# Scores in causal blocks and states in channel blocks on the column groups of the matmul array

## The chip, the cores and the metric

The kernel runs on one core of a Trainium2 chip. The core has a matrix engine (PE in the profile; its weight loads are shown as PEld), a vector engine (DVE), a scalar engine (ACT), GpSimd (POOL) and SP, which here issues all the kernel's DMAs. The metric is the device time of one execution in microseconds; lower is better.

## The reference, cut to what matters

The program is a gated linear recurrence (4 batches, 8 heads, 768 steps, 48 channels per head), followed by a feed-forward network with a product of two branches. In the recurrence, a state of 48 x 48 per head is turned and shrunk by a complex gate at each step, receives the outer product of k and v, and is read by q.

```python
mag = np.sqrt(a_re * a_re + a_im * a_im)
scale = np.minimum(mag, 0.999) / (mag + 1e-06)
a_re_n, a_im_n = (a_re * scale, a_im * scale)
for t in range(S):
    ar, ai = (a_re_n[:, :, t, :, None], a_im_n[:, :, t, :, None])
    new_re = ar * S_re - ai * S_im
    new_im = ar * S_im + ai * S_re
    kv = np.einsum('bhd,bhe->bhde', k[:, :, t], v[:, :, t])
    S_re, S_im = (new_re + kv, new_im)
    y[:, :, t] = np.einsum('bhd,bhde->bhe', q[:, :, t], S_re)
# then, with x = y as (3072, 384):
h = (x @ w1) * (x @ w2) @ w3
return (h @ w_out).astype(np.float32)
```

## The kernel before

The kernel computes the recurrence in closed form. The running product of the gates is taken out of the sum: q is multiplied by it, k is divided by it, and both become vectors of 96 numbers per step and head (real and imaginary parts of 48 channels). Then y is the causal part of a score matrix (k against q) times v, plus q times a state that is carried from chunk to chunk. A chunk is C = 128 steps. A unit u is half a batch: all 8 heads (H) over TT = 384 steps, so UC = 3 chunks; there are NU = 8 units.

For each unit, `gates` (from line 541) computes the gates' products with a long chain of operations that alternates between ACT and DVE. Its last product for k is gR, line 634. `move` (line 648) then copies the results from a layout of 3 tiles of 128 partitions into QL and KL, where the 96 channels of one head lie on 96 partitions. The recurrence's work on PE comes in pieces, listed by `pieces` (line 1005):

- `turn` transposes k's two parts (line 671); ACT copies the result to KT (line 673).
- `state` (line 714) multiplies, for each head, KT (128 steps x 96 channels as weights) with v, whose head is padded to 64 columns (line 721), and adds the result to the carried state T (line 728); after the last chunk of a unit T is scaled (line 734). In the second unit of a batch the last chunk needs no state, so a batch has 5 state chunks.
- `scores` (line 676) is called twice for a chunk, with x = 0 and 1, for 4 heads each: one product per head of 128 keys (weights) with 128 queries (line 683). DVE copies the part that the mask `causal` allows into A (line 685); A was cleared once, so what is not allowed stays zero.
- `outputs` (line 691) multiplies A with v and T with q, in pieces of 32 output channels that go to four different ranges of 32 output partitions (line 710). The head's 48 channels and 16 zeros make two such pieces; QUADS says which pieces of two neighbouring heads are summed in one place. An even head has its 48 channels first, an odd head has them last. ACT copies the sum to xT (line 712).

The v of a unit is loaded with one DMA into vr (line 517, `load_v`, called in `load_qkv`); ACT spreads it into the padded V with two copies (line 524, `spread_v`, called in `gates`). vr has one buffer, V has two.

The feed-forward network of a unit (lines 744 to 750, and 795 or 831 for its output) follows one unit behind. `unit` (line 1026) interleaves on PE its pieces with the recurrence's pieces, and issues a step of the next unit's `gates` after each. PE's order is thus written out by hand (`manual_schedule`, line 1042). On the other engines and on SP the framework's planner orders the instructions, by its own estimates of cost and by priority; the copies out of PE's results are marked as of high priority. At the start, the weights of the network are converted from double precision, and w3 and w_out are multiplied together (`fuse`, line 968, into eight accumulators in PSUM, two of them from the pool of the scores). In later units `check_weights` (line 899) loads weights once more ("look") and checks ranges on ACT (lines 918 to 921).

Of the kernel before, what the change touches and what calls it, by code (L numbers as in the profile page):

```python
# [13 lines left out]
U16 = mybir.dt.uint16  # L14
BF = mybir.dt.bfloat16
# [359 lines left out]
def kernel(  # L375
# [55 lines left out]
    LO, HI = 32, D - 32  # L431
    LN_EPS = math.log(1e-6)
# [16 lines left out]
    three = fast.enter_context(tc.tile_pool(name="three", bufs=3))  # L449
    ps_s = fast.enter_context(tc.tile_pool(name="ps_s", bufs=2, space=PSUM))  # L450
# [6 lines left out]

    Ab = [singles.tile([P, H, C], FP, name=f"A{i}") for i in range(2)]
# [3 lines left out]
    causal = singles.tile([P, C], I32, name="causal")  # L462
    nc.gpsimd.iota(causal, pattern=[[1, C]], base=0, channel_multiplier=-1)
    nc.vector.tensor_scalar(out=causal, in0=causal, scalar1=0, scalar2=None, op0=OP.is_ge)
# [37 lines left out]
    def load_qkv(u):  # L502
        b, h = divmod(u, 2)
        if "q" not in g_t.get(u, {}):
            take_qk(u)
        g = g_t[u]
        load_rows(g["k"], kt, u)
        load_rows(g["q"], qt, u)
        if u:
            load_v(u)  # L510
# [9 lines left out]
    def spread_v(u):  # L520
        vr = g_t[u]["vr"].rearrange("p c (h two d) -> p c h two d", two=2, d=D)
        V = Vb[u % 2].rearrange("p c (h two) e -> p c h two e", two=2)
        for i, e0 in enumerate((0, 64 - D)):
            nc.scalar.copy(out=V[:, :, :, i, e0:e0 + D], in_=vr[:, :, :, i])
# [16 lines left out]
    def gates(u, split):  # L541
# [64 lines left out]
        if u:  # L606
            spread_v(u)
# [68 lines left out]
    def scores(u, c, x):  # L676
# [4 lines left out]
        sc = ps_s.tile([P, n, C], FP, tag="sc", name="sc")  # L681
        for j in range(n):
            nc.tensor.matmul(out=sc[:, j], lhsT=KL[:, x * n + j, w], rhs=QL[:, x * n + j, w], start=True, stop=True)  # L683
        with tc.high_priority():
            masked[:] = [nc.vector.copy_predicated(out=A[:, x * n:(x + 1) * n], data=sc,  # L685
                                      mask=causal.rearrange("p (h t) -> p h t", h=1).to_broadcast([P, n, C]))]


    QUADS = [q for h in range(0, H, 2) for q in ([(h, 0)], [(h, 1), (h + 1, 0)], [(h + 1, 1)])]

    def outputs(u, c):
# [9 lines left out]
        for i, q in enumerate(QUADS):  # L701
            f, j = divmod(i, 4)
            o = y[32 * j:32 * j + 32, f]
            got = [(V[:, hd, 32 * e:32 * e + 32], A[:, hd]) for hd, e in q]
            if not first:
                got += [(T[:, hd, 32 * e:32 * e + 32], QL[:, hd, w]) for hd, e in q]
# [6 lines left out]

    def state(u, c):

        KT, V = KT_t.pop((u, c)), Vb[u % 2][:, c]
        n = u % 2 * UC + c
        T = T_t.get((u // 2, n))
        kv = ps_v.tile([2 * D, H, 64], FP, tag="v", name="kv")
        for hd in range(H):  # L720
            nc.tensor.matmul(out=kv[:, hd], lhsT=KT[:, hd].rearrange("p d x f -> p (d x f)"), rhs=V[:, hd],  # L721
                             start=True, stop=True)
        Tn = three.tile([2 * D, H, 64], FP, tag="T", name="T")
        with tc.high_priority():
            if T is None:
                nc.scalar.copy(out=Tn, in_=kv)
            else:
                add = nc.vector.tensor_tensor(out=Tn, in0=kv, in1=T, op=OP.add)  # L728
# [3 lines left out]
        if c == UC - 1:  # L732
            rho = L_t[u][1][:, :, TT:TT + 1].to_broadcast([2 * D, H, 64])
            nc.vector.tensor_tensor(out=Tn, in0=Tn, in1=rho, op=OP.mult)
        T_t[u // 2, n + 1] = Tn

# [231 lines left out]
    def fuse(f, j):  # L968
        if not sums:
            sums.extend([ps_s.tile([P, DM], FP, tag="sc", name="f") for _ in range(2)] +  # L970
# [71 lines left out]
    with tc.manual_schedule(engines={mybir.EngineType.PE}):  # L1042
# [9 lines left out]
        for f in range(KF):  # L1052
# [5 lines left out]
            if f == VLOAD:  # L1058
                load_v(0)
            if f >= KF - 2:  # L1060
# [8 lines left out]
        spread_v(0)  # L1069
# [10 lines left out]
        for i, p in enumerate(pieces(0)):  # L1080
# [4 lines left out]
            if i == 0:  # L1085
                for f in work[:2]:
                    f()
                load_qkv(1)
            for _ in range(5 if i == 0 else i >= 6):
# [17 lines left out]
        for u in range(1, NU):  # L1107
            steps = gates(u + 1, False) if u + 1 < NU else iter(())
# [49 lines left out]
```

## Time and profile before

| | |
|---|---|
| median of 3 runs | 569.44 us (569.23 to 571.16) |
| profiled execution, its span | 566.8 us (the page gives no other time for it) |
| PE busy | 541.8 us (96%) |
| PEld busy | 386.1 us (68%) |
| DVE busy | 335.8 us (59%) |
| ACT busy | 345.9 us (61%) |
| POOL busy | 3.5 us (1%) |
| DMA | 84.74 MB, mean 150 GB/s |

The page counts an engine as busy while at least one of its instructions runs, so matmuls that run at the same time in different column groups count once. A row of a group gives the line, the engine, the operation, the tiles (written <- read), the shape, the number of records, the busy time in microseconds, the mean duration of one in nanoseconds, the idle time before it, and what ended that. One float32 product leaves two matmul records and two weight-load records. The mean duration of a matmul is its whole way through the array and is longer than the distance to the next one. In the chain of work that ended last, each entry has its start, its length on the chain and its instructions; a PE entry's length there is the distance to what follows, which is what a stage costs.

### The profile page before, as it was taken

How to read it: one execution, taken by the hardware profiler on the slowest of the kernel's cores; microseconds unless marked ns; L12 is line 12 of the kernel's file. 1: busy time of each engine (PE TensorE's matmuls, PEld its weight loads, DVE VectorE, ACT ScalarE, POOL GpSimd, SP SyncE). 2: the span in 40 equal slices, each digit the busy share in tenths (PEclk: the TensorE clock that was granted, in tenths of full speed). 3: DMA queues.
4: the chain of work that ended last, by engine and by line, in shares of the span. 5: the costliest groups of instructions: out<-in, count | busy, mean ns of one | idle time of the engine just before them, and what ended most of it. 6: DMA issues, size and time to landing. Idle time of an engine off the chain costs nothing.

```text
span 566.8 us, 9285 instructions
## 1 busy us (share of the span) xinstructions
PE 541.8 (96%) x3682; PEld 386.1 (68%) x3682; DVE 335.8 (59%) x511; ACT 345.9 (61%) x569; POOL 3.5 (1%) x9
## 2 busy tenths in 40 slices
PE   4697899999999999999999999999999999999995
PEld 2354775577566975688567966697568965796564
DVE  6998599927752677356742796255743696332121
ACT  6979856655662798458963899289965645101100
POOL 2000000000000000000000000000000000000000
PEclk9999999999999999999999999999999999999999
DMA  8996985780382447935593427754393104200001
GB/s 285 374 364 190 322 268 169 204 214 16 98 189 53 122 141 221 247 109 183 184 206 111 144 81 218 209 157 148 125 207 101 30 28 115 67 2 30 0 1 47
DMA packets 46772, 84.74 MB, mean 150 GB/s; under 512 B 4736, under 2 KB 36480, under 8 KB 45952
## 3 DMA queue, kind: packets, MB, share of 16 engines
q1 hardware_dynamic: 46720, 84.06, 50.6%
q8 instruction: 31, 0.51, 0.4%
q14 instruction: 21, 0.17, 0.1%
HBM read 60.42 MB, written 4.72 MB: 115 GB/s over the span
## 4 chain that ended last, share of the span: by engine, by line
PE 77%; ACT 9%; DVE 7%; DMA 3%; issue 2%; SPq 1%; DVEq 0%; ACTq 0%
PE m L744 40%; PE o L831 9%; PE p L795 9%; PE y L710 5%; PE sc L683 5%; PE kv L721 5%; PE tp L671 2%; ACT gZ L554 1%; DMA look<-in_w_dram 1%; ACT look L918 1%; ACT look L919 1%; PE f L973 1%; DMA im<-in_a_im_dram 1%; ACT gR L554 1%; ACT gA L554 1%
## 5 line engine op out<-in xcount | busy, mean ns | idle before, releaser
L744 PE MATMUL m<-xT,w1s 128*128 128x384 f32 x384 | 135.0, 488 | 0.1
L744 PE MATMUL m<-xT,w2s 128*128 128x384 f32 x384 | 134.3, 486 | 0.0
L744 PEld LDWEIGHTS m<-xT,w2s 128*128 128x128 f32 x384 | 73.0, 190 | 50.9
L744 PEld LDWEIGHTS m<-xT,w1s 128*128 128x128 f32 x384 | 71.2, 190 | 45.3 <-ACT xT L712 1.0
L750 DVE TENSOR_TENSOR ab<-m,a 128x384 f32<-128x384 f32 x64 | 35.2, 553 | 84.7 <-PE m L744 77.4
L749 ACT COPY a<-m 128x384 f32<-128x384 f32 x64 | 30.1, 474 | 53.5 <-PE m L744 52.3
L973 PE MATMUL f<-wo_s,w3s 128*128 128x384 f32 x128 | 47.7, 528 | 15.5 <-DVE wo_s L887 15.5
L831 PE MATMUL o<-w3o,ab 128*128 128x384 f32 x160 | 54.0, 487 | 0.0
L673 ACT COPY KT<-tp 128x384 f32<-128x384 f32 x40 | 33.6, 851 | 32.2 <-PE tp L671 32.1
L973 PEld LDWEIGHTS f<-wo_s,w3s 128*128 128x128 f32 x128 | 25.5, 206 | 35.2 <-DVE wo_s L887 18.6
L683 PE MATMUL sc<-QL,KL 96*128 96x128 f32 x384 | 47.2, 276 | 0.3 <-DVE A L685 0.3
L683 PEld LDWEIGHTS sc<-QL,KL 96*128 96x128 f32 x384 | 45.7, 192 | 1.3 <-DVE A L685 0.6
L685 DVE COPY_PREDICATED A<-causal,sc 128x512 f32<-128x512 int32 x48 | 34.6, 741 | 14.0 <-PE sc L683 13.6
L831 PEld LDWEIGHTS o<-w3o,ab 128*128 128x128 f32 x160 | 29.6, 190 | 18.7 <-issue 0.4
L728 DVE TENSOR_TENSOR T<-kv,T 96x512 f32<-96x512 f32 x16 | 11.0, 686 | 51.4 <-PE kv L721 51.4
L710 PE MATMUL y<-A,V 128*32 128x128 f32 x768 | 39.2, 275 | 0.0
L710 PEld LDWEIGHTS y<-A,V 128*32 128x32 f32 x768 | 32.9, 109 | 3.3 <-issue 1.4
L710 PE MATMUL y<-QL,T 96*32 96x128 f32 x640 | 34.4, 272 | 0.0
L877 ACT ACTIVATE low<-raw 128x384 uint16<-128x384 uint32 (+4 forms) x28 | 25.1, 902 | 11.1 <-DVE low L873 5.1
L721 PEld LDWEIGHTS kv<-V,KT 128*96 128x96 f32 x320 | 29.6, 165 | 3.1 <-issue 1.4
L795 PE MATMUL p<-To,So 128*128 128x192 f32 x168 | 31.6, 335 | 0.0
L721 PE MATMUL kv<-V,KT 128*96 128x64 f32 x320 | 30.0, 247 | 1.5 <-ACT KT L673 1.5
(114 smaller groups left out, 748.7 us busy)
## 6 DMA issues: line engine op xcount, KB each, us to landing
look<-in_w_dram SPq DMA_DIRECT2D x28, 512.0 KB, 3.9
raw<-in_w_dram SPq DMA_DIRECT2D x6, 1024.0 KB, 10.2
raw<-in_w_dram SPq DMA_DIRECT2D x8, 768.0 KB, 6.7
KL<-gR SPq DMA_DIRECT2D x24, 192.5 KB, 3.3
KL<-k SPq DMA_DIRECT2D x24, 192.5 KB, 3.8
re<-in_a_re_dram SPq DMA_DIRECT2D x24, 192.0 KB, 5.2
im<-in_a_im_dram SPq DMA_DIRECT2D x24, 192.0 KB, 3.2
k<-in_k_dram SPq DMA_DIRECT2D x24, 192.0 KB, 3.3
```

The lines of the kernel that those rows point to most:

```text
L673: nc.scalar.copy(out=KT_t[u, c][:, :, :, x].rearrange("p h d f -> p f d h"), in_=tp.rearrange("p f (d h) -> p f d h", h=H))
L683: nc.tensor.matmul(out=sc[:, j], lhsT=KL[:, x * n + j, w], rhs=QL[:, x * n + j, w], start=True, stop=True)
L685: masked[:] = [nc.vector.copy_predicated(out=A[:, x * n:(x + 1) * n], data=sc, mask=causal.rearrange("p (h t) -> p h t", h=1).to_broadcast ...
L710: nc.tensor.matmul(out=o, lhsT=a, rhs=b, start=s0, stop=s1)
L721: nc.tensor.matmul(out=kv[:, hd], lhsT=KT[:, hd].rearrange("p d x f -> p (d x f)"), rhs=V[:, hd], start=True, stop=True)
L744: nc.tensor.matmul(out=m, lhsT=w[:, j * P // WB, f, j * P % WB:j * P % WB + P], rhs=xT_t[u][:, f], start=(f == 0), stop=(f == KD - 1))
L749: copied[:] = [nc.scalar.copy(out=a, in_=got[0])]
L750: nc.vector.tensor_tensor(out=ab_t[u][:, j], in0=got[1], in1=a, op=OP.mult)
L795: nc.tensor.matmul(out=m[p], lhsT=a[:, f], rhs=b[:, f], start=(f == 0), stop=(f == KH - 1))
L831: nc.tensor.matmul(out=m, lhsT=ab_t[u][:, f, t * P:(t + 1) * P], rhs=w3o[:, f], start=(f == 0), stop=(f == KF - 1))
L877: nc.scalar.activation(out=ends.bitcast(U16)[:, 0::2].rearrange("p (r m) -> p r m", r=r), in_=lo.bitcast(U32), func=AF.Copy, scale=2.0 ** -29)
L973: nc.tensor.matmul(out=sums[j], lhsT=w3_t[f][:, j * P:(j + 1) * P], rhs=w3_t["wo"][:, f], start=(f == 0), stop=(f == KF - 1))
```

## The change

Scores. The 128 keys of a chunk are taken in four blocks of 32 (SB). A block that starts at key s0 is multiplied only with the queries from s0 on, so the four blocks have 128, 96, 64 and 32 columns. The result of a block goes to one of four ranges of 32 PSUM partitions, g = (s0 / 32 + j) mod 4 for head j of the four, so four products in a row, of four heads, go to four different ranges. The keys of head j are therefore rotated by 32 j partitions in the scores and in A. The two PSUM tiles Sc are allocated and cleared once, and the mask becomes one byte per element, for four rotations.

States. The 96 channels of a head are taken as three blocks of 32, which go to three ranges of PSUM partitions. They read v from vr, unpadded (48 columns), and T is kept in three fixed tiles that were cleared once.

v. `turn_v` loads v a second time, straight into V, rotated per head as the scores are: one or two DMAs per head, 14 per unit, in rows of 48 numbers. `spread_v` goes. Every head now has its 48 channels first; for an odd head `part` takes the 16 zeros from the end of the head before. `load_v` is issued after the unit's last state, and `turn_v` of unit u + 1 at the beginning of unit u.

```diff
-    three = fast.enter_context(tc.tile_pool(name="three", bufs=3))
-    ps_s = fast.enter_context(tc.tile_pool(name="ps_s", bufs=2, space=PSUM))
+    ps_s = fast.enter_context(tc.tile_pool(name="ps_s", bufs=1, space=PSUM))
...
+    Sc = [ps_s.tile([P, LANES, C], FP, name=f"sc{i}") for i in range(2)]
+    for sc in Sc:
+        nc.vector.memset(sc, 0.0)
...
-    causal = singles.tile([P, C], I32, name="causal")
-    nc.gpsimd.iota(causal, pattern=[[1, C]], base=0, channel_multiplier=-1)
-    nc.vector.tensor_scalar(out=causal, in0=causal, scalar1=0, scalar2=None, op0=OP.is_ge)
+    causal = one.tile([P, LANES, C], I32, tag="q", name="causal")
+    nc.gpsimd.iota(causal, pattern=[[SB, LANES], [1, C]], base=0, channel_multiplier=-1)
+    for j in range(1, LANES):
+        nc.vector.tensor_scalar(out=causal[0:SB * j, j], in0=causal[0:SB * j, j], scalar1=-C, scalar2=None, op0=OP.add)
+    mask = singles.tile([P, LANES, C], U8, name="mask")
+    nc.vector.tensor_scalar(out=mask, in0=causal, scalar1=0, scalar2=None, op0=OP.is_ge)
...
-    def spread_v(u):
-        vr = g_t[u]["vr"].rearrange("p c (h two d) -> p c h two d", two=2, d=D)
-        V = Vb[u % 2].rearrange("p c (h two) e -> p c h two e", two=2)
-        for i, e0 in enumerate((0, 64 - D)):
-            nc.scalar.copy(out=V[:, :, :, i, e0:e0 + D], in_=vr[:, :, :, i])
+    def turn_v(u):
+        b, h = divmod(u, 2)
+        src = v[b, h * TT:(h + 1) * TT].rearrange("(c p) (h d) -> p c h d", p=C, d=D)
+        for hd in range(H):
+            r = SB * (hd % LANES)
+            for p0, p1, s0 in ((r, C, 0), (0, r, C - r)):
+                if p1 > p0:
+                    nc.sync.dma_start(out=Vb[u % 2][p0:p1, :, hd, 0:D], in_=src[s0:s0 + p1 - p0, :, hd])
...
-        sc = ps_s.tile([P, n, C], FP, tag="sc", name="sc")
-        for j in range(n):
-            nc.tensor.matmul(out=sc[:, j], lhsT=KL[:, x * n + j, w], rhs=QL[:, x * n + j, w], start=True, stop=True)
+        sc = Sc[x]
+        for s0 in SPANS:
+            for j in range(n):
+                g = (s0 // SB + j) % LANES
+                nc.tensor.matmul(out=sc[SB * g:SB * g + SB, j, s0:C], lhsT=KL[:, x * n + j, w][:, s0:s0 + SB],
+                                 rhs=QL[:, x * n + j, w][:, s0:C], start=True, stop=True)
...
+    SPANS = (0, 3 * SB, SB, 2 * SB)
...
+    def part(X, hd, e):
+
+        e0 = 64 * hd + 32 * e - (64 - D) * (hd % 2)
+        return X.rearrange("p h e -> p (h e)")[:, e0:e0 + 32]
...
+    Tb = [singles.tile([2 * D, H, 64], FP, name=f"T{i}") for i in range(3)]
+    for T in Tb:
+        nc.gpsimd.memset(T, 0.0)
...
-        KT, V = KT_t.pop((u, c)), Vb[u % 2][:, c]
+        KT, V = KT_t.pop((u, c)), g_t[u]["vr"][:, c].rearrange("p (h d) -> p h d", d=D)
...
-            nc.tensor.matmul(out=kv[:, hd], lhsT=KT[:, hd].rearrange("p d x f -> p (d x f)"), rhs=V[:, hd],
-                             start=True, stop=True)
-        Tn = three.tile([2 * D, H, 64], FP, tag="T", name="T")
+            rows = KT[:, hd].rearrange("p d x f -> p (d x f)")
+            for g in range(0, 2 * D, SB):
+                nc.tensor.matmul(out=kv[g:g + SB, hd], lhsT=rows[:, g:g + SB], rhs=V[:, hd], start=True, stop=True)
+        Tn = Tb[(u * UC + c) % 3]
...
-                add = nc.vector.tensor_tensor(out=Tn, in0=kv, in1=T, op=OP.add)
+                add = nc.vector.tensor_tensor(out=Tn[:, :, 0:D], in0=kv, in1=T[:, :, 0:D], op=OP.add)
...
+        if u + 1 < NU and c == UC - 1 - u % 2:
+            load_v(u + 1)
...
             if f == VLOAD:
                 load_v(0)
+                turn_v(0)
...
                 load_qkv(1)
+                turn_v(1)
...
         for u in range(1, NU):
+            if u + 1 < NU:
+                turn_v(u + 1)
```

## The prediction

> **What bounds the kernel now.** I read the page first, for the engines' shares and the costliest groups.
>
> ```profile
> PE 541.8 (96%) x3682; PEld 386.1 (68%) x3682; DVE 335.8 (59%) x511; ACT 345.9 (61%) x569; POOL 3.5 (1%) x9
> L683 PE MATMUL sc<-QL,KL 96*128 96x128 f32 x384 | 47.2, 276 | 0.3 <-DVE A L685 0.3
> L721 PEld LDWEIGHTS kv<-V,KT 128*96 128x96 f32 x320 | 29.6, 165 | 3.1 <-issue 1.4
> L721 PE MATMUL kv<-V,KT 128*96 128x64 f32 x320 | 30.0, 247 | 1.5 <-ACT KT L673 1.5
> q1 hardware_dynamic: 46720, 84.06, 50.6%
> ```
>
> The matmul engine works 96% of the span, and two of its groups, scores (L683) and states (L721), are what the change rewrites. A float32 product leaves two records: 24 chunks x 8 heads are 192 score products, x384. I call one record with its weight load a pair. Next, the table by stage, to see where PE is short of work.
>
> ```profile
> 0.00:55.00 55.00, 39.47 (x106) 21.77 (x107) 49.03 (x111) 46.81 (x78) 3.53 (x9) 0.97 0.88 308
> 55.00:82.00 27.00, 25.14 (x300) 20.08 (x299) 19.03 (x29) 19.73 (x28) 0.00 (x0) 1.00 0.94 284
> 205.00:266.00 61.00, 61.00 (x454) 44.88 (x453) 36.70 (x50) 43.30 (x73) 0.00 (x0) 1.00 0.64 185
> 391.00:453.00 62.00, 60.61 (x435) 44.35 (x434) 36.65 (x50) 44.00 (x77) 0.00 (x0) 1.00 0.44 119
> ```
>
> The columns after the length are PE, weight load, DVE, ACT and POOL, then clock, DMA share and GB/s. From 82 us to 515 us PE is busy all the time but for some 1.5 us; up to 55 us DVE and ACT rule. So a microsecond off PE after 82 us is a microsecond off the span, until something else is late. The chain gives each stage's real length (first start to the next stage's first start); unit 2's end:
>
> ```profile
> 187.27 1.33 PE kv L721 x16
> 188.60 1.84 PE sc L683 x16
> 190.44 1.30 PE p L795 x8
> 191.74 1.79 PE sc L683 x16
> 193.53 1.01 PE y L710 x32
> 194.54 1.50 PE p L795 x8
> ...
> 197.82 1.89 PE y L710 x64
> ...
> 409.83 1.37 DVE gR L634
> 411.20 0.14 issue
> 411.34 0.52 PE tp L671 x3
> ```
>
> Scores: 1.79 us for 16 pairs, 112 ns for 128 columns. States: 1.33 for 16, 83 ns for only 64 columns. The outputs y, whose weights are 32 columns wide in four column groups, take (1.89 - 1.01) / 32 = 27.5 ns a pair for 128 columns, a quarter of 110. The last three lines are the rival clock: in unit 6 the transposes wait for the gates' last product. Lastly, the matmul timeline at the ends of y:
>
> ```profile
> 191.58 1.95 PE L683 MATMUL sc<-QL,KL 96*128 96x128 f32 x16
> 193.46 1.08 PE L710 MATMUL y<-A,V 128*32 128x128 f32 x32
> 194.47 1.57 PE L795 MATMUL p<-To,So 128*128 128x192 f32 x8
> 500.60 0.43 PE L710 MATMUL y<-A,V 128*32 128x128 f32 x8
> ```
>
> Scores that precede y last 193.46 - 191.58 = 1.88 us, not 1.79: entering four groups costs 0.09. y's 32 pairs are 8 per group at 0.11 = 0.875 us, but 1.01 pass: 0.14 for start and end. A visit to the narrow mode costs 0.23 us. In the last line the first four matmuls start at 500.604, .611, .617 and .624, each with its weight load, and the next four 0.13 us later: four groups start 7 ns apart and then each waits for its own stream.
>
> **What the Trainium skill says.** "TensorE: Matmul & The Clock Gate", section "LDWEIGHTS (loading the stationary operand)", prices a weight load by its columns at 1.2 GHz: 96 are 80 ns (the trace's 83 for a state pair agrees: states are bound by weights, not by 64 columns), 32 are 27. The same page, "Wait — 56ns, not 53.3ns?", says that start-to-start never drops below about 25 ns however short the product; the trace's 7 ns between groups says this isn't so across groups, but no row shows whether 7 ns can last. "TensorEngine Tiling (Array Packing)", "Key Properties", says that changing the tiling mode drains the engine: the 0.23 us agrees. "DMA: Bandwidth & Descriptors", "Specifications", puts the least size for full rate at 512 B; the new v rows are 192 B, and the trace has no such packet.
>
> **The change part by part.** Columns: 112 ns / 128 and 322 / 384 (L744, 12 in 3.87 us) give 0.83 ns a column and about 3 ns a pair.
>
> Scores. Per half (4 heads) each group gets a block of 128, 32, 96 and 64 columns, two pairs each: 110 + 32 (the 32-column weight load rules) + 83 + 56 = 281 ns, twice, 0.56 us. Both halves: 1.12 against 1.79; 0.67 x 24 = 16.0 us off.
>
> States. 8 heads x 3 blocks x 2 pairs in three groups: 16 pairs per group, 48 columns, 43 ns each (40 + 3, over 32 for weights): 0.69 us against 1.33; 0.64 x 20 = 12.9 off.
>
> Mode visits. In the chain's order states stand alone (or just before the first scores), scores 1 and 2 stand before y. Units 2 to 7 go from 3 visits to 6, unit 1 from 2 to 3, unit 0 from 2 to 5: 22 more, x 0.23 = 5.0 on.
>
> Dispatch. 64 pairs in 1.12 us are 17.5 ns each, 48 in 0.69 are 14.3. Sustained supply is known to be at least one in 27.5; bursts 7. I take it as hidden: PE's sequencer is seen issuing the scores' semaphore waits at 245.1 to 245.4 us, some 20 pairs before the scores start at 247.25, so a backlog exists when a stage begins.
>
> So PE gains 23.9. Unit 0 (3.3 of it) lies in 55 to 82 us, where PE idles 1.9 us waiting for ACT and DVE; I count 1.2, between 0 and 3.3. That leaves 21.8.
>
> The gates. The product gR (L634) ends before its transposes by 8.8, 6.0, 1.8, 2.5, 1.4, 0.1 and 0.6 us in units 1 to 7. Its chain of some 36 to 40 us starts behind an ACT copy that PE releases just before the scores; in that stretch PE gets about 1.8 us faster. Units 5 to 7 then wait 0.4 + 1.7 + 1.2 = 3.3 us at most. Against it: the two copies of v (L524, 0.67 us each) leave ACT, and one sits at 265.9 us just ahead of this chain's exp. I take 1.5 lost. The gone copies, 10.5 us of ACT, else earn nothing; the narrower state sums on DVE (384 for 512 columns, 0.69 to about 0.55 us, x20) lie under PE.
>
> v twice. Per unit 14 more DMAs on SP at 0.41 (vr's issue) to 0.60 us (k's): 5.7 to 8.4. In 203.65 to 223.38 us SP issues for about 5 us of 20, and unit u+1's turned v is free to load since y of unit u-1, so it fits; what stands behind it in SP's order are looks, the im loads and the KL moves. The moves land 5 to 28 us before their scores. Looks are worse: ACT takes them in order, and a late one holds the copies behind it. 3072 packets of 192 B per unit: by today's mean (50.6% x 566.8 x 16 / 46720 = 98 ns for 1.8 KB) at most 98, by bytes at least 10 ns: 2 to 19 us of queue per unit; I take 30 ns, 6 us, hidden by 50 us of lead. With y's new waits on these loads I charge 1.5 us in all, 0 to 8. The plain v load moves behind the unit's last state (its buffer is now read there), over 30 us before its next use.
>
> The start. On DVE two PSUM clears, three mask adds and the mask itself: from A's clear (0.91 us for 1024) and the old mask's 0.22, about 2 us, in the first 10 us where DVE has some 3 us of gaps; 0.5 (0 to 2). Turned v of unit 0 goes behind v at 30.3 us, where SP waits until 41.5: hidden. The longer memsets and iota on POOL are hidden, since it has nothing else to do.
>
> The masked copies (0.74 us) read a byte mask, which no row shows; as little as a 128x512 sum (0.69) or up to twice as much, they end before the next chunk's scores, 3 us later. I count none.
>
> Sum: 21.8 - 1.5 - 1.5 - 0.5 = 18.3. Span 566.8 - 18.3 = 548.5. The page gives only the span; the median of the runs is 569.4, 2.6 more, so 551.
>
> **Rivals.** (a) The gain is half given back: ACT, DVE or SP in their new planned order run late, so PE waits at the transposes and at xT. For: 0.1 and 0.6 us of slack, ACT loaded 70% by unit. Against: ACT loses 1.3 us of work per unit. With unit 0 giving nothing, the gates, the loads and the start at their worst, 23.9 - 3.3 - 3.3 - 8 - 2 = 7.3 are left: 562. With reordered copies on top, 555 to 566.
>
> (b) Dispatch or the 25 ns floor binds. 2496 new pairs replace 24 x 1.79 + 20 x 1.33 = 69.6 us. With the 5.0 of visits, break-even lies at (69.6 - 5.0) / 2496 = 25.9 ns a pair. At 25 ns it gains 2 us, no change; at 27.5, all that is proven to last, products take 68.6, and it loses 4.0: 573; with the gates untouched and the 2 us of start and loads, 575. This is the side on which it ends slower. Against: the 7 ns bursts.
>
> (c) The change does not do what it says, blocks of one row falling into one group and running in turn: a score chunk would take four times 1.12 and a state chunk three times 0.69, adding 2.7 x 24 + 0.7 x 20 = 79 us. The start partitions written (32g) are y's own form, which does run fourfold, so I give it almost nothing.
>
> **How the numbers follow.** The forecast (546 to 555) 0.60, (a) 0.22, no change within 0.5% (2.8 us, what a measurement of this kernel can tell) 0.06, (b) and (c) slower 0.12. The floor, 545, is all of PE's 23.9. The top, 568, takes in (a) and part of no change. Faster: 0.60 + 0.22 = 0.82.
>
> **What would show it.** Scores near 1.1 to 1.2 us per chunk and states near 0.7 to 0.9 in the chain; if they stand at 1.6 and 1.2 or more, (b) holds. Groups starting 7 ns apart in the timeline. For (a): waits of tp on gR and of m on xT above 3 us. If SP's waits or DMA ahead of ACT's looks grow by several us a unit, my charge for v was too small.

## The result, and the profile after

| | before | after |
|---|---|---|
| median of the runs, us | 569.84 (4 runs, 569.23 to 571.16) | 561.12 (4 runs, 560.75 to 562.18) |
| profiled execution's span, us | 566.8 | 559.5 |
| first transposition of units 0 and 1, us | 57.31, 115.19 | 55.78, 118.23 |
| units 1 to 7 to the end of the span, us | 451.6 | 441.3 |

The ratio is 0.9846, with a 95% interval of 0.9816 to 0.9875: faster, by 8.7 us. The forecast was 551.0, a gain of 18.4. The sign and the range (545 to 568) held; more than half of the gain is missing.

The page of the changed kernel first: engine shares, the rewritten groups, the DMA queues.

```profile
PE 525.5 (94%) x5474; PEld 359.1 (64%) x5474; DVE 334.8 (60%) x516; ACT 338.0 (60%) x553; POOL 5.2 (1%) x12
L691 PE MATMUL sc<-QL,KL 96*32 96x64 f32 (+3 forms) x1536 | 33.8, 238 | 6.6 <-DVE A L694 3.0
q1 hardware_dynamic: 73088, 88.79, 58.0%
q8 instruction: 45, 0.74, 0.6%
```

TensorE is busy 16.3 us less, as wanted, but it now waits: 94% instead of 96%. Its scores have 6.6 us of idle time ahead of them where they had 0.3. It has 5474 products instead of 3682, and instruction fetches rose from 31 to 45. The chain of the changed kernel (start, length, what) in unit 2, and where it turns to the gates in unit 6:

```profile
189.05 0.81 PE kv L742 x48
...
191.20 1.50 PE p L817 x8
192.70 1.25 PE sc L691 x64
193.95 0.92 PE y L725 x32
...
406.76 1.37 DVE gR L640
...
408.27 0.52 PE tp L677 x3
```

A state chunk takes 0.81 us for 48 pairs, 16.9 ns a pair (before: 1.33). A score chunk takes 1.18 on average (3.54 for the three of a unit, as the matmul timeline adds up; before 1.79), 18 ns a pair, and its four groups start 5 to 8 ns apart in that timeline. So the matmul side does what was meant. Look at p between two score chunks: its 8 products take 1.50 us where they took 1.30. The table by stage, columns as before (PE, weight load, DVE, ACT, POOL, clock, DMA share, GB/s):

```profile
55.00:82.00 27.00, 20.61 (x488) 15.80 (x490) 17.05 (x27) 18.02 (x23) 0.00 (x0) 0.87 0.99 259
205.00:266.00 61.00, 58.98 (x660) 41.03 (x659) 37.47 (x51) 44.51 (x74) 0.00 (x0) 1.00 0.71 194
391.00:453.00 62.00, 61.73 (x690) 43.16 (x689) 37.99 (x52) 42.24 (x71) 0.00 (x0) 1.00 0.50 137
```

Two places lose. In 55 to 82 us, which is unit 0, PE is busy 20.6 us instead of 25.1, and its clock is 0.87 instead of 1.00. In 205 to 266 us, where PE had not one idle moment, it idles 2.0 us. PE's waits after 82 us (total, times, longest) name that second loss:

```profile
PE tp L677 <- DVE gR L640: 3.1, 4, 1.3
PE m L766 <- ACT xT L727: 1.8, 2, 1.1
PE sc L691 <- issue: 1.4, 3, 0.8
PE y L725 <- issue: 0.4, 1, 0.4
```

Before, the only wait there was 1.4 us on gR. The waits of 55 to 82 us name the first loss:

```profile
PE sc L691 <- DVE A L694: 2.7, 2, 2.2
PE sc L691 <- DMA QL<-q: 2.2, 1, 2.2
PE kv L742 <- ACT KT L679: 1.1, 1, 1.1
```

The second line is the moves of q's rotated rows, which the forecast had landing early. SyncE's own timeline (start, length, issues) shows why they are late. After:

```profile
32.76 16.41 SPq L532 DMA_DIRECT2D V<-in_v_dram  x14
49.27 1.85 SPq L494 DMA_DIRECT2D re<-in_a_re_dram  x3
...
53.13 0.63 SPq L654 DMA_DIRECT2D KL<-gR  x1
...
60.87 0.55 SPq L654 DMA_DIRECT2D QL<-q  x1
```

And before:

```profile
41.54 1.83 SPq L487 DMA_DIRECT2D re<-in_a_re_dram  x3
...
45.39 1.51 SPq L648 DMA_DIRECT2D KL<-gR  x1
...
57.48 0.56 SPq L648 DMA_DIRECT2D QL<-q  x1
```

The 14 transfers of turned v hold SyncE from 32.8 to 49.2 us, where 14 x 0.6 = 8.4 had been reckoned to fit ahead of 41.5. None of the 14 is issued before the eighth transfer ahead of it on this queue has landed, and six of them are issued within 0.1 us of that landing; for the first eight of them that eighth is a weight block or v itself, which here land 8 to 13 us after their issue. These waits make 5.6 of the 16.4 us. The other 10.8 are the issues themselves: two of them take 1.6 and 3.1 us instead of 0.6, which stays unexplained. Everything behind starts late: the loads of re and the first move by 7.7 us, the last move by 3.4, and the last of QL lands at 67.3 us instead of 60.8.

The third thing is the clock. PE's clock by the microsecond in the changed kernel (length, busy, clock, DMA share, GB/s):

```profile
66.00:67.00 1.00, 0.00 (x0) 1.00 1.05 326
67.00:68.00 1.00, 0.61 (x29) 0.90 1.05 387
68.00:69.00 1.00, 1.00 (x39) 0.50 1.04 383
69.00:70.00 1.00, 1.00 (x17) 0.50 1.05 387
70.00:71.00 1.00, 1.00 (x3) 0.50 1.06 389
71.00:72.00 1.00, 1.00 (x11) 0.89 1.12 401
```

After the idle stretch of 2.2 us the clock is halved for 3.4 us (0.2 + 3 + 0.2), half of which, 1.7 us, is work that PE does not get done. It happens again at 78.0 to 81.5 us, behind the second wait. Before, the clock in this stretch was 1.00 throughout.

When it happens can be read more closely. In every trace the half clock begins and, but at the trace's end, ends on a grid of 3.413 us steps; the two stretches here begin 10.24 us, three steps, apart. These are the two steps ahead of them (length, busy, clock, DMA share, GB/s):

```profile
64.40:67.81 3.41, 1.22 (x72) 1.00 1.06 297
74.64:78.05 3.41, 1.24 (x68) 1.00 1.09 239
```

PE is busy for 36% of each. Over all 20 kept traces, from 50 us on, every step at full clock in which PE was busy, by the profile, less than 44% was followed by a step at half clock (45 of 45), and none in which it was busy more than 51%; in between it went both ways. So it is the busy share of such a step that decides, not the length of one wait, and where the grid falls against the program differs from one trace to the next.

### The profile page after: what moved, and what is told of

Its sections match the earlier page's. It is cut to its first block, busy times and chain, and to the rows that moved or that the text cites. A ratio compares the mean times of both kernels' runs of the same rounds, so it can differ in the third digit from the quotient of the medians.

```text
span 559.5 us, 13023 instructions
## 1 busy us (share of the span) xinstructions
PE 525.5 (94%) x5474; PEld 359.1 (64%) x5474; DVE 334.8 (60%) x516; ACT 338.0 (60%) x553; POOL 5.2 (1%) x12
## 4 chain that ended last, share of the span: by engine, by line
PE 53%; DVE 18%; ACT 16%; issue 5%; DMA 4%; SPq 2%; DVEq 0%; ACTq 0%
PE m L766 26%; PE o L853 8%; PE p L817 7%; PE y L725 4%; PE sc L691 4%; ACT gZ L562 3%; ACT re L562 3%; DVE gA L598 3%; DVE gZ L621 2%; PE kv L742 2%; ACT gR L562 2%; PE tp L677 2%; ACT gA L562 2%; ACT low L899 1%; DVE gR L640 1%
## 5 line engine op out<-in xcount | busy, mean ns | idle before, releaser
L771 ACT COPY a<-m 128x384 f32<-128x384 f32 x64 | 30.3, 475 | 53.9 <-PE m L766 52.7
L694 DVE COPY_PREDICATED A<-mask,sc 128x512 f32<-128x512 uint8 x48 | 33.2, 730 | 14.6 <-PE sc L691 14.4
L691 PE MATMUL sc<-QL,KL 96*32 96x64 f32 (+3 forms) x1536 | 33.8, 238 | 6.6 <-DVE A L694 3.0
L691 PEld LDWEIGHTS sc<-QL,KL 96*32 96x32 f32 x1536 | 29.1, 112 | 13.0 <-issue 5.1
L725 PE MATMUL y<-QL,T 96*32 96x128 f32 x640 | 36.6, 280 | 0.4 <-issue 0.4
L995 PE MATMUL f<-wo_s,w3s 128*128 128x384 f32 x96 | 36.6, 528 | 0.0
L725 PEld LDWEIGHTS y<-A,V 128*32 128x32 f32 x768 | 34.7, 112 | 1.4 <-issue 1.4
L748 DVE TENSOR_TENSOR T<-kv,T 96x384 f32<-96x384 f32 x16 | 8.8, 553 | 43.6 <-PE kv L742 43.4
L725 PEld LDWEIGHTS y<-QL,T 96*32 96x32 f32 x640 | 32.6, 113 | 0.9 <-issue 0.9
L995 PEld LDWEIGHTS f<-wo_s,w3s 128*128 128x128 f32 x96 | 20.0, 212 | 14.3 <-issue 4.5
L817 PEld LDWEIGHTS p<-To,So 128*128 128x128 f32 x168 | 27.0, 190 | 3.2 <-issue 3.0
```

Source lines behind the costliest of these rows:

```text
L691: nc.tensor.matmul(out=sc[SB * g:SB * g + SB, j, s0:C], lhsT=KL[:, x * n + j, w][:, s0:s0 + SB], rhs=QL[:, x * n + j, w][:, s0:C], start=T ...
L725: nc.tensor.matmul(out=o, lhsT=a, rhs=b, start=s0, stop=s1)
L771: copied[:] = [nc.scalar.copy(out=a, in_=got[0])]
L817: nc.tensor.matmul(out=m[p], lhsT=a[:, f], rhs=b[:, f], start=(f == 0), stop=(f == KH - 1))
L995: nc.tensor.matmul(out=sums[j], lhsT=w3_t[f][:, j * P:(j + 1) * P], rhs=w3_t["wo"][:, f], start=(f == 0), stop=(f == KF - 1))
```

## The experiments

Theories at the outset. S: turned v at the start stands ahead of moves and weights on SyncE's queue. D: it isn't the order but the full DMA engines. G: from unit 2 on, the gates' chain, which PE's shorter products don't shorten, gives the gain back. When S and D both failed for unit 0, a fourth came in, U: in unit 0 the others set the pace, and a faster PE idles and falls to half clock.

**Each part alone.** The kernel before, with v loaded a second time, turned, by the same transfers at the same places, in place of ScalarE's spread:

```diff
-        if u:
-            spread_v(u)
...
             if f == VLOAD:
                 load_v(0)
+                turn_v(0)
```

> The kernel before with nothing but the loads of v changed: the two ACT copies go, and 14 DMAs per unit bring v into its padded place, of the same sizes and at the same places of the program as in the change (no rotation; the load to vr stays, without a reader). The prediction's charge for v, for its gains on ACT and for the start gives 569 to 572. Theory S: 575 to 580, nearly all of it lost before 85 us. Rival P: 569 to 571.

Measured: 579.92 us against 569.61, ratio 1.0177 (1.0156 to 1.0198), slower by 10.3. The first transposition comes at 60.2 us (57.3), that of unit 1 at 126.8 (115.2); from there on the two kernels take the same time within 1.1 us. SyncE and PE (waits of 55 to 130 us) of this run:

```profile
31.17 16.87 SPq L534 DMA_DIRECT2D V<-in_v_dram  x14
48.14 1.84 SPq L487 DMA_DIRECT2D re<-in_a_re_dram  x3
74.43 9.74 SPq L534 DMA_DIRECT2D V<-in_v_dram  x14
84.28 3.82 SPq L866 DMA_DIRECT2D raw<-in_w_dram  x4
```

```profile
PE f L981 <- DVE wo_s L895: 2.9, 1, 2.9
PE m L752 <- DVE w2s L895: 2.7, 1, 2.7
```

Unit 1's transfers, in turn, stand ahead of the last blocks of w1 and w2 (84.3 us; 74.6 before), and the FFN of unit 0 waits for them: m takes 36.2 us instead of 31.0. The clock is at half for 17.1 us between 54 and 112 us, here with whole products. The second load of v is thus, by itself, not a charge of 1.5 us but of 10.3, all of it before unit 1. Against this kernel the changed one is 18.8 us faster: that is what the blocks bring once v is loaded twice.

The changed kernel with whole states, then with whole scores (v then needs no rotation, and its second load is 8 transfers a unit instead of 14):

```diff
-            for g in range(0, 2 * D, SB):
-                nc.tensor.matmul(out=kv[g:g + SB, hd], lhsT=rows[:, g:g + SB], rhs=V[:, hd], ...)
+            nc.tensor.matmul(out=kv[:, hd], lhsT=rows, rhs=V[:, hd], start=True, stop=True)
```

> The changed kernel with the states as whole products of 96 channels again (48 columns, v from vr); scores stay in blocks. A state chunk goes back from 0.81 us and about 0.2 for changing the mode to about 1.33. If PE is the bound everywhere, as the prediction has it, 20 chunks x 0.3 to 0.4 = 6 to 8 us slower than the changed kernel, 567 to 569. If the gates' chain and the copies now set the time of the units (theory G), less than half of it shows: 562 to 565.

```diff
-        for s0 in SPANS:
-            for j in range(n):
...
+        for j in range(n):
+            nc.tensor.matmul(out=sc[:, j], lhsT=KL[:, x * n + j, w], rhs=QL[:, x * n + j, w], ...)
```

> The changed kernel with whole score products of 128 keys and 128 queries again, an unrotated mask and v turned by no partitions (8 DMAs per unit, not 14); states stay in blocks. If PE is the bound, a score chunk goes back from 1.14 to 1.79 us: 24 x 0.65 = 15 us slower, less what three visits per unit to the narrow mode cost (some 2 us) and what 48 DMAs fewer give: 569 to 574. Under theory G and S, part of the waits goes with the faster scores and fewer DMAs: 563 to 568.

Measured: whole states 566.53 against 569.61 (ratio 0.9944, 0.9923 to 0.9964), whole scores 562.56 (0.9871, 0.9844 to 0.9898). The first lies between its two forecasts, the second below both. By the medians the changed kernel loses 5.4 us without the states' blocks and only 1.4 without the scores' blocks; the 1.4 is not clear of noise, since its interval overlaps the changed kernel's. In the kernel with whole scores PE's waits after 82 us are these and no others:

```profile
PE m L761 <- ACT xT L722: 1.0, 1, 1.0
PE tp L675 <- ACT KT L677: 0.2, 1, 0.2
```

The wait on gR is gone. In units 1 to 7 of this profile (of the slowest of its four runs) the scores take 11.9 us more, but the stages m, at whose ends the waits for gR lie, take 4.5 less, p between scores that are wide again 2.8 less and y 0.8 less; these units are 3.6 us longer in all. So the slower scores fill time that PE otherwise waits, and save visits to the narrow mode. The first fits G: the gates' chain starts just ahead of the scores, so what the scores gain falls inside it, while the states come before it. Unit 0 takes 60.4 us (62.5 in the changed kernel) but starts 2.3 later. So 1.4 is not the worth of the scores by themselves.

**Where turned v stands (S against D).** Unit 0's turned v behind unit 0's moves:

```diff
                 load_v(0)
-                turn_v(0)
...
+        turn_v(0)
         for f in work[:2]:
```

> The changed kernel, with only the first unit's turned v moved: its 14 DMAs are issued after the first unit's moves to KL and QL, not before the second unit's gate loads. Theory S (the 14 DMAs hold SP from 32.8 to 49.2 us at the start, so the gate loads and the moves of the first units come 7.7 us later, and the products of unit 0 wait and collide): the moves start near 45 us again, the feed-forward products of unit 0 start near 79 to 81 us and not 84.7, and the time falls by 3.5 to 6 us, to 555 to 558. Rival P (unit 0 is long because DVE and ACT can't follow the faster score and state blocks): the moves start earlier, but unit 0 stays as long and the time stays at 560 to 562.

Measured: 566.11 against 569.61 (0.9963, 0.9927 to 0.9999). A miss, and slower than the changed kernel. The moves start at 48.4 us instead of 53.1, but now the 14 transfers (57.4 to 67.3 us) stand ahead of w1 and w2, which go out at 67.4 instead of 61.5 and with the last block at 90.7; unit 0 takes 66.0 us. All turned v on GpSimd's queue:

```diff
-                    nc.sync.dma_start(out=Vb[u % 2][p0:p1, :, hd, 0:D], in_=src[...])
+                    nc.gpsimd.dma_start(out=Vb[u % 2][p0:p1, :, hd, 0:D], in_=src[...])
```

> The changed kernel with all loads of the turned v issued by POOL on its own queue, not by SP; POOL has nothing else to do after the start. Theory S (SP's order is what makes the second load of v dear at the start, 11.6 us in the run with v twice alone): SP's moves for unit 0 start near 45 us again, the loads of w1 and w2 and of the gates don't wait, and 115 to 118 us of the first part become 110 to 113: 553 to 557 in all. Rival D (it is the DMA engines themselves, which are full at the start and are given 6144 small packets more): the first part stays at 117 to 120 us and the time at 559 to 563.

Measured: 568.0 against 569.68 (0.9965, 0.9951 to 0.9979), slower than both forecasts. GpSimd issues both units' v at 6 to 30 us, in among the first weights; the first transposition is at 61.6 us, 5.9 later than in the changed kernel. SyncE's order is free here and the start is later all the same, which speaks for DMA time; it was not isolated. Behind the weights instead (unit 0's after the second block of w1 and w2, unit 1's after the last):

> The changed kernel with the 14 transfers of turned v moved down the same queue: unit 0's behind the fetch of the second block of w1 and w2, unit 1's behind the last block. Theory (turned v stands on the queue ahead of the gates' loads, the moves and the weights, and each transfer waits for the eighth before it to land): the moves start by 46 us again, the first transposition of unit 1 comes at 112 to 115 us (118.2 in the changed kernel), 555 to 558 us. Rival (its packets cost the same wherever they stand): 560 to 564 us.

Measured: 568.77 against 569.72 (0.9981, 0.997 to 0.9992), a miss: moves at 49.7 us, but the transfers then run from 61.1 to 76.7 us, y waits for V 2.5 us and 7.0 for masked scores, and unit 0 takes 70.6 us. On GpSimd's queue again, each unit's transfers now held back by a small write to V that needs the end of unit 0's gates, or unit 0's first output:

```diff
+            nc.gpsimd.tensor_scalar(out=Vb[u % 2][:, :, :, 0], in0=after, scalar1=0.0, scalar2=None, op0=OP.mult)
...
+        turn_v(0, nc.gpsimd, g_t[0]["Z"][:, :, 0:H])
...
+        turn_v(1, nc.gpsimd, xT_t[0][:, :, 0:H])
```

> The changed kernel with turned v of units 0 and 1 on GpSimd's queue, held until the gates of unit 0 are done and until unit 0's first output is copied, so that it neither stands on SyncE's queue nor runs while the first weights land. Theory (order at the start, not the bytes): the first transposition of unit 1 at 111 to 114 us, 553 to 557 us. Rival (28 more transfers cost DMA time wherever they are): 560 to 564 us.

Measured: 563.39 against 569.72 (0.9887, 0.9858 to 0.9916): the rival's range. SyncE's queue is free and the weights no longer wait (m 30.96 us), and still unit 0 takes 64.4 us. So neither order nor place was enough. PE's waits in 55 to 86 us of this run:

```profile
PE y L728 <- issue: 2.4, 1, 2.4
PE kv L745 <- ACT KT L682: 2.3, 2, 2.1
```

These are other waits than the changed kernel's, of the same size.

**Without any second load (U).** The blocks of four different key ranges run side by side instead of four heads with turned rows, so v needs no turning and is loaded once and spread by ScalarE, as before:

```diff
-        for s0 in SPANS:
-            for j in range(n):
-                g = (s0 // SB + j) % LANES
+        for i in range(n):
+            for j in range(n):
+                s0 = SPANS[(i + j) % n]
+                g = s0 // SB
```

> The changed kernel without turned v: the four products that run side by side are of four different blocks of keys instead of four heads with turned rows, so the rows of v stay where they are, v is loaded once, and ScalarE spreads it as in the kernel before (one copy of 128x1152 a unit). Theory (the second load of v at the start eats the gain of unit 0 and more): the first transposition of unit 1 at 110 to 114 us (118.2 in the changed kernel), a score chunk at most 1.5 us, 551 to 555 us. Rival (unit 0 is held by the moves, ScalarE and VectorE whatever v does): first transposition at 116 to 118 us, 557 to 561 us.

Two kernels beside it, with the same order of blocks: v loaded a second time in three transfers a unit instead of 14, and v loaded only that way.

> The same order of blocks without turned rows, but v loaded a second time as in the changed kernel, at the same places, in three transfers a unit instead of fourteen: same bytes and packets. If the number of transfers on the queue is what costs: first transposition of unit 1 at 111 to 115 us, 552 to 556 us. If the packets cost: as the changed kernel, 118 us and 560 to 562 us.

> As the kernel with three transfers, and the first load of v left out: the state products read the same tile. Half the bytes of v. If the bytes matter at the start, 1 to 2 us below the kernel with three transfers; if not, the same within 0.5 us.

Measured: 572.38, 573.62 and 575.7 against 569.54 (ratios 1.0037, 1.0053, 1.0085, each within 0.0024). All three miss both of their forecasts. Two readings. First, the edit ties each block to one column group (`g = s0 // SB`), so one group gets every block of 128 columns. Its 16 pairs of a chunk follow each other at 109 ns in the matmul timeline and fill the whole stage, while the other groups have less to do: 5.0 us for the three score chunks of a unit instead of 3.54, which costs some 8 us in units 1 to 7. Spreading the lengths evenly over the groups is what the turned rows are for. Second, unit 0 takes 64.1, 64.5 and 65.7 us although the first of them has no second load at all, and at most 2.3 us of it is the slower scores. Fewer transfers or fewer bytes brought nothing: v once, by three transfers, was by the medians even 2 us slower than twice, with intervals that overlap. The clock is not all of it either: the kernel with v twice in three transfers has no half clock between 55 and 121 us, and its unit 0 takes 64.5 us. PE's waits in 55 to 86 us of the kernel with v loaded once and spread:

```profile
PE y L723 <- issue: 2.8, 1, 2.8
PE kv L740 <- ACT KT L676: 2.3, 2, 2.1
```

With the blocks, PE is ready for the third state at 64 us and waits until 66.1 for ScalarE's copy of the transposes; before, it asked at 65.9 and got it at 66.8. The clock behind that wait:

```profile
65.00:66.00 1.00, 0.00 (x0) 0.94 1.05 387
66.00:67.00 1.00, 0.92 (x36) 0.50 1.07 389
67.00:68.00 1.00, 1.00 (x43) 0.50 1.07 323
```

**The clock by itself.** Seven products ahead of unit 0's first scores, to keep PE busy while it waits for the moves:

```diff
+        if (u, c, x) == (0, 0, 0):
+            for i in range(7):
+                nc.tensor.matmul(out=sc...[:, 0:DM], lhsT=ident, rhs=g_t[0]["vr"][:, 0], ...)
```

> The changed kernel with seven products of 128x384 (0.32 us each) put on TensorE ahead of unit 0's first scores, where it waits 2.2 us for the moves; their result is overwritten. Theory (an idle stretch of two us is followed by some 3.4 us at half clock, which doubles the price of the wait): the granted clock of 67 to 72 us is 1.00 instead of 0.50, the scores and the fusing products after it take 1.2 and 1.3 us instead of 2.0 and 2.4, the first transposition of unit 1 comes 1 to 2 us earlier (118.2), 559 to 560.5 us in all. Rival (the clock falls for another reason): clock and times as in the changed kernel, 561 us.

Measured: 561.14 against 569.54 (0.9832, 0.9788 to 0.9875), the same total as the changed kernel: the forecast in time missed, the one of the clock came true. The filler was twice as long as meant: a float32 product leaves two records, so seven are 4.7 us, and the scores start at 69.6 us, 2.2 later than without it. In spite of that the first transposition of unit 1 comes 0.6 us earlier. The clock, in its own trace:

```profile
68.00:69.00 1.00, 1.00 (x5) 1.00 1.04 381
69.00:70.00 1.00, 1.00 (x26) 1.00 1.06 389
70.00:71.00 1.00, 1.00 (x56) 1.00 1.06 391
```

The first scores take 1.25 us (1.96 in the changed kernel) and the fusing products after them 1.49 (2.40). So idleness is what halves the clock, and keeping PE busy gained back the 2.2 us that the filler took, and 0.6 more. The next wait, 2.05 us long, was not followed by half clock. It fell across two steps of the grid, and PE was busy for 71 and 69% of them:

```profile
72.09:75.51 3.42, 2.42 (x97) 1.00 1.07 297
75.51:78.92 3.41, 2.36 (x108) 1.00 0.98 228
```

**The blocks undone in unit 0 alone.** Whole products and ScalarE's spread of v in unit 0; units 1 to 7 as in the changed kernel. GpSimd zeroes the A tiles again before unit 1.

```diff
+        for j in range(n if u == 0 else 0):
+            nc.tensor.matmul(out=sc[:, j], lhsT=KL[:, x * n + j, w], rhs=QL[:, x * n + j, w], ...)
+        for s0 in SPANS if u else ():
...
-                turn_v(0)
...
+        nc.scalar.copy(out=Vb[0][:, :, :, 0:D], in_=g_t[0]["vr"].rearrange("p c (h d) -> p c h d", d=D))
...
+        for A in Ab:
+            nc.gpsimd.memset(A, 0.0)
```

> The changed kernel with the change undone in unit 0 alone: its scores and states are whole products again, its v is spread by ScalarE without a second load; the A tiles are zeroed again after it. Units 1 to 7 as in the changed kernel, turned v of unit 1 at its place on SyncE's queue. Theory (in unit 0, ScalarE, VectorE, the moves and the fetches of instructions set the pace; shorter products only make TensorE idle and then run at half clock): no half clock between 57 and 82 us, unit 0 takes 57.5 to 59 us (62.5 in the changed kernel, 57.9 before), 556 to 558 us in all. Rival (unit 0 loses its time to something else in the changed kernel): 61 us or more for unit 0, 560 to 562 us.

> As the kernel before, and turned v of unit 1 on GpSimd's queue, held until unit 0's first output is copied. If the 14 transfers of unit 1 on SyncE's queue still delay unit 0 and its weights: another 1 to 2 us less, 555 to 557 us; if not, the same within 0.5 us.

Measured: 558.7 (0.9801, 0.9778 to 0.9824) and 557.73 (0.9785, 0.9763 to 0.9807) against 569.55. By their medians both are faster than the changed kernel, by 2.4 and 3.4 us; the first's interval overlaps the changed kernel's, the second's lies wholly below it. The first just misses its forecasts (558.7 for 558, unit 0 59.3 for 59). The stretch of unit 0 in the first of them, columns as in the table by stage:

```profile
55.00:82.00 27.00, 24.36 (x296) 19.49 (x295) 19.44 (x28) 19.18 (x27) 1.91 (x2) 1.00 0.87 233
```

The clock is 1.00, PE idles 2.6 us instead of 6.4, and unit 0 takes 59.3 us (62.5 changed, 57.9 before). The first transposition of unit 1 comes at 115.3 us, as before the change (115.2; 118.2 changed). This trace is of the fastest of five executions: two, with a mean clock of 0.995 and 0.997, took 556.2 and 557.1 us, and three, with 0.988 and 0.989, took 558.7 to 559.6, so in those the clock did fall somewhere. What unit 0 has left over 57.9 is mostly in m, 32.1 us instead of 31.0. The second kernel was to bring that back; its unit 0 took 60.3, with m at 33.1, waiting 1.4 us for VectorE. That expectation missed, and the two kernels can't be told apart by their times.

**The gates (G).** The range checks on the inputs and weights left out, from the changed kernel and from the one before; ScalarE is then busy 30.4 us instead of 44.5 in 205 to 266 us of the changed kernel.

> The changed kernel without the second look at the weights and gates (the range checks on ACT from unit 2 on are left out, with their loads). ACT loses some 13 us per unit in units 2 to 6, so the gates' chain gets shorter and less of it queues. Theory G (in units 2 to 7 PE waits for gR at the transposes, slack 0.15 us in four of five, so the gain of the faster scores is swallowed): the waits of tp on gR and of m on xT go, and the time falls by 5 to 7 us: 554 to 556. Rival I (the lost time is PE's own: changes of mode and late instructions): at most 2 us faster, 559 to 561.

> The kernel before without the same looks, for comparison. PE has only some 2 us of waits after 82 us here, so both theories: 0.5 to 2.5 us faster than before, 567 to 569.

Measured: 559.14 against 569.68 (0.9812, 0.978 to 0.9845), and 568.94 (0.9982, 0.997 to 0.9994). By the medians the changed kernel gains 2.0 us by it (the intervals overlap), the one before 0.7. That is the rival's range, not theory G's. In the profile units 1 to 7 are 3.1 us shorter, and unit 0 0.8 longer, with the clock at half for 10.2 us of it. PE's waits after 82 us:

```profile
PE m L766 <- ACT xT L727: 3.4, 2, 1.8
PE sc L691 <- issue: 1.3, 2, 1.1
```

The 3.1 us on gR are gone, and half of them are back at xT. Two edits that were to shorten the gates' chain don't decide it. The product of q with the decay moved behind the chain:

> The changed kernel with one operation of the gates' chain moved, for units 2 to 7: the product of q with the decay (DVE, 1.35 us), which stands before the products for k, is done later, when DVE waits for ACT's sines. Nothing is left out. Theory G: the chain from its first logarithm to gR gets up to 1.35 us shorter, the slack at the transposes returns in part, and 3 to 5 us are gained: 556 to 558. Rival I: no change, 560 to 562.

561.35 against 569.68 (0.9853, 0.9826 to 0.9879), the rival's range. But PE waits on gR 3.1 us as before: the edit did not bring gR forward, so it doesn't test what an earlier gR is worth. The load of re and the first logarithm earlier, alone and together with turned v on GpSimd's queue:

> The changed kernel with the gates' re of the next unit loaded between the moves of KL and of QL, and its first logarithm on ScalarE after the first copy of the FFN, so that the chain of the gates ends well before the next unit's transpositions. Theory (the gates' chain gives the scores' gain back from unit 2 on): TensorE's waits on gR and xT together fall from 4.9 us to under 1.5, 555 to 558 us. Rival (the gain went into the narrow visits and their instruction fetches, and the waits only change their name): 559 to 562 us.

> The two edits before together: turned v of units 0 and 1 on GpSimd's queue, held, and the gates early. If the two causes are separate their gains add: 548 to 552 us, near the 551 of the prediction. If the start only hides what comes later: 554 to 558 us.

651.67 and 652.5 against 569.72 (1.142 and 1.1473). The planner laid out everything anew, and PE's waits of the first (after 82 us) show where it went:

```profile
PE sc L695 <- DVE A L698: 60.5, 6, 31.0
```

That tells nothing of G. An ordering edit in a planned kernel is a different plan, and its time can't be laid to the edit.

## Why the prediction was right or wrong

**Scores (1.12 for 1.79) and states (0.69 for 1.33): right.** 1.14 to 1.25 and 0.81. The pairs of one group in a state follow each other at 43 ns, as forecast; what 0.81 has above 0.69 is the stage's start and end, which the forecast counts with the visit. By stage, from the start of each to the start of the next, units 1 to 7 spent 39.2 us on scores before and 27.5 after, 22.6 on states and 14.4: 20.0 us off, of 25.0 forecast for those units. Of the missing 5.0, 2.7 are in the states, nearly all of it such starts and ends, and 2.3 are in the scores of units 1 and 4, whose three chunks take 5.0 and 4.8 us with stalls inside.

**Dispatch as hidden, the 7 ns bursts: right.** 16.9 ns a pair lasts for 48 pairs, 18 ns for 64. Rival (b), which needed 25.9, is out, and so is the floor of about 25 ns that the Trainium skill gives ("TensorE: Matmul & The Clock Gate", "Wait — 56ns, not 53.3ns?"): it doesn't hold across column groups.

**192-byte packets at 30 ns: cheaper, 18 ns on average. The mask: right,** 730 ns for the masked copy with a byte mask (741 with the old one).

**Mode visits at 0.23 us: too small.** The stage behind a narrow one is slower too: p between two of them takes 1.50 instead of 1.30 us, and only half of the 0.20, the entry, was in the 0.23. In units 1 to 7 the stages beside the narrow ones (p, transposes, o, m) take 4.4 us more apart from waits, and with the 2.7 in the states the 19 visits cost 7.1 us instead of 4.4: 0.37 each, 2.7 us more than forecast. It was there to be read before: the forecast's own fence has p behind a y at 1.50, and at 1.30 between scores (from start to start, 1.40 and 1.30; the chain, which the forecast read as going from start to start, goes by ends).

**"Turned v of unit 0 goes behind v at 30.3 us, where SP waits until 41.5: hidden": the step that failed.** It put the transfers of unit 0 at nothing, and all of v twice at 1.5 us; alone, v twice costs 10.3 us. The issue times were right for the later units (0.5 to 0.6 us each, 7 to 8 for the 14). What was left out is that at the start a transfer waits for the landing of the eighth before it, on DMA engines that were 88% busy already: 16.4 us instead of at most 8.4, over the end of the gap and into the moves, and from there into unit 0.

**Unit 0 gains 1.2 "between 0 and 3.3": wrong in sign.** It lost 4.6, and the whole start with it 3.0 (the first transposition came 1.5 us earlier). The bound was at fault: a unit in which PE already waits for others was taken to gain nothing at worst. In fact PE waited again, for late moves, the masked copies and ScalarE's copy, idled two us at a time, and each such wait could be followed by 3.4 us at half clock. The Trainium skill has the mechanism ("TensorE: Matmul & The Clock Gate", "What's actually happening": a half-rate idle state, left after a busy window of about 3.4 us, with windows that run freely). The trace agrees, with 3.4 us at 0.50 each time. The same page's section "HAM oscillation — how this bites in real kernels" warns of gaps above 3.4 us; here 2.1 to 2.2 us sufficed where they fell into one step of 3.41 us and left PE busy for less than 44% of it, and 2.05 us that fell across two steps did not. The forecast cites the page for other things and prices no idle stretch.

Is it v or the blocks? Either alone makes unit 0 late: v twice with whole products 66.6 us, blocks with a single load of v 64.1 (some 2.3 of it the slower order), both 62.5, and 59.3 with both undone there. They don't add, and taking away one alone returned nothing, so the 10.3 can't be counted as v's share of the changed kernel's loss; that they use up the same slack is the reading that fits. That part of the blocks' loss is the fetch of instructions, of which PE now needs half as many again, is argued and not shown: stalls without a releaser of 2.4 and 2.8 us stand in unit 0 of two kernels with blocks, and those of the changed kernel after 82 us, like the one of 2.4, end 1.4 to 1.7 us behind the end of an instruction fetch.

**Gates, 1.5 us of at most 3.3: mis-sized, mechanism right.** 3.1 us on gR instead of 1.4, 1.8 on xT, 0.3 on VectorE's products: 3.8 us more than before, and 4.6 in the lengths of the stages that end in these waits. The bound of 3.3 had only gR in it; xT, named under rival (a), came on top. Without the range checks, gR's share went and xT's grew, which fits that PE now runs into ScalarE and VectorE as a whole, not into one instruction; no run isolates it.

The sum redone, by stage: 20.6 us were forecast for PE in units 1 to 7. Less 2.7 for the visits, 2.3 for the stalls in the scores, 4.6 for the gates and xT, and 0.8 in y (0.4 of it a stall), 10.2 are left, and 10.3 were measured there. The start and unit 0, forecast at 1.2 - 0.5 = 0.7 gained, lost 3.0. Together 7.3 in the profiled spans, of 18.3: 11.0 are missing. Of these 3.7 lie before unit 1, where the mechanism was wrong. The other 7.3, in units 1 to 7, are sizes: 3.1 at the gates and xT beyond the 1.5, 2.7 for the visits, 2.3 and 0.8 for the stalls and y, less the 1.5 charged for v, which these units don't show (7.4, within the rounding). Rival (a) is what happened, by its number and in part by its cause: its waits at the transposes and xT are there, 4.9 us, but more was lost before unit 1 and to PE's own visits and stalls.

## What to carry to other kernels

Before a faster stage is counted as a gain, ask where each of its instructions will wait when it comes early: a stage that others hold up can end later than before, and idle time can be paid again at half clock. Count a transfer put in a queue's gap with what it itself must wait for, not by its issue time, and look at what stands behind it. Where a change helps in most stages and hurts in one, undo it in that one: here that took 561.1 to 558.7 and 557.7.

## What the runs showed of the hardware

- TensorE's clock fell to 0.50 in steps of 3.413 us. It fell after every such step in which PE had been busy less than 44% (45 of 45 in 20 traces), after none above 51%; two idle stretches of 2.2 us in unit 0 did it, and seven products of filler kept it at 1.00.
- Matmuls of several column groups keep up 17 ns a pair over 48 pairs (three groups) and 18 ns over 64 (four) if every group gets the same columns in all. When one group got all the blocks of 128 columns, its pairs at 109 ns set the length of the stage: 26 ns a pair.
- In this program no transfer at the start was issued on SyncE's queue before the eighth ahead of it had landed: 14 small transfers behind large ones took 16.4 us there, those for units 2 and 3 took 8.4 and 8.7.
- Leaving the narrow mode slows the next stage by 0.1 us: 8 products of p take 1.30 us from start to start between wide stages, 1.40 beside one narrow stage and 1.50 between two.
